# Order of the first normalisation, of the last q tile and of the reciprocal loads in an adaLN block with linear attention and SwiGLU

## The chip, the cores and the metric

The kernel runs on one core of a Trainium2 chip. The metric is the device time of one execution in microseconds, the median of several. All times below are in microseconds (us) unless they are marked ns.

## The reference

One block of a conditioned transformer over 2048 tokens of 1024 features, in bf16: an adaptive layer norm, linear attention with 32 heads of 32 features, a gated residual, a second adaptive layer norm, a SwiGLU feed-forward part with 3584 hidden features, and a second gated residual.

```python
def _layernorm(x, axis=-1, eps=1e-05):
    m = jnp.mean(x, axis=axis, keepdims=True)
    v = jnp.var(x, axis=axis, keepdims=True)
    return (x - m) / jnp.sqrt(v + eps)

def _A_ref(x, wqkv, wo):                     # H = 32 heads
    q, k, v = heads_of(x @ wqkv)
    phi = lambda t: jnp.where(t > 0, t + 1, jnp.exp(t)) + 1e-06
    pq, pk = (phi(q), phi(k))
    kv = jnp.einsum('bhsd,bhse->bhde', pk, v)
    z = jnp.einsum('bhsd->bhd', pk)
    num = jnp.einsum('bhqd,bhde->bhqe', pq, kv)
    den = jnp.einsum('bhqd,bhd->bhq', pq, z)[..., None] + 1e-06
    return merge(num / den) @ wo

def _B_ref(x, w_gate, w_up, w_down):
    return _silu(x @ w_gate) * (x @ w_up) @ w_down

x = A_x
mod = (_silu(c) @ w_mod).reshape(c.shape[0], 6, 1, -1)
sa, ca, ga, sb, cb, gb = (mod[:, i] for i in range(6))
h = _layernorm(x, axis=-1) * (1 + ca) + sa
x = x + ga * _A_ref(h, A_wqkv, A_wo)
h = _layernorm(x, axis=-1) * (1 + cb) + sb
x = x + gb * _B_ref(h, B_w_gate, B_w_up, B_w_down)
```

(`heads_of` and `merge` stand here for the reshapes and transposes.)

## The kernel before

**Engines and order.** Every instruction goes through a small recorder, the class `_Prog`. It appends it to the list of its engine, works out from the memory it touches which earlier instructions it must wait for, and later emits the five lists with semaphore waits. So each engine works in exactly the order in which the Python code calls it, and all lines of the profile are the recorder's line 176. SP issues nearly all DMAs in the order of the calls; `P.wait_for("sp", ...)` makes SP stand until the named instructions are done, and whatever is queued on SP behind it stands too. A PSUM bank is guarded as a whole: an engine that touches it waits for the last access of the other engines.

**Tiling.** The 2048 tokens are 16 row tiles of 128 and four chunks of 512. The 1024 features are 8 tiles of 128, called `dt` where they are summed over and `nt` where they are made. `XRES` holds x and then its norm, `HT` two chunks of h transposed (features on the partitions), `WQK` and `WV` the weights, `PQT` phi(q) transposed, `PKT` and `PKH` phi(k).

**Head.** SP loads row tiles 0 to 3, then the weights of the modulation and of q. TensorE runs filler products (`warm`) on a zeroed tile. Tiles 0 and 2 get mean and variance on VectorE (`s0_`, `s2_`: two halves with `bn_stats`, then an aggregate), tiles 1 and 3 on ScalarE (`act_stats`: a pass for the sum, a pass for the squares; `msq_neg` and `ve_sums` make the variance). POOL computes (variance + eps) to the power −1/2 for one tile at a time (`ln1_rstd1`, `pool_pow`), VectorE applies the norm (`ln1_xn`, `ln1_xn_sum`), and TensorE turns the tile into PSUM with eight products against the identity (`tile_transposes`). Between the turns, `mod_sc` computes columns of the scale 1 + ca: 8 products of one column for each feature tile `m`. `fin_ca` writes them to `MODCOL`, and `h0_first` scales the turned tiles into `HT`.

**q of chunk 0** (`q_phase_chunk0`). The sum over `dt` is taken in pieces for q tiles 0 to 6, each in its own PSUM bank (`qb`), as weights and scales arrive; the shift sa is computed meanwhile (`mod_sc(WSA, ...)`), all in bank 0. Features 0 to 3 enter without their shift, and the missing share is put into a bias (`bias_mm`, `bias_fin`), after which `h0_shift` adds the shift to `HT`. The eighth q tile (`nt` 7) has no bank left: it comes last, in bank 0, after the bias has been read from it. `q_phi` evacuates each tile twice on ScalarE (exp and relu, with the bias), `q_min` and `q_add` make phi(q) from them on VectorE. In the same stretch the rows 4 to 7 of chunk 1 are normalised and transposed by DMA (`th_dma`).

**k, and chunks 1 to 3.** `k_group` and `q_group` make one tile of k or q with eight products of 512 columns; `next_bank` gives the bank in a fixed rotation. `kside`, `s1`, `s2` and `s3` are lists written out by hand: which other work is called after which group. `th_mod` applies scale and shift to a transposed chunk, `ln_half` computes sums for a later chunk, `macc` sums another part of the modulation.

**G and the attention output.** `g_group` makes G = x normᵀ · phi(k) in 16 groups, `g_evac` writes each. `den` computes the denominators, writes their reciprocals to DRAM (`RDR`) and reads them back, each row broadcast to 32 partitions, into `RB`: eight DMAs in two groups of four feature tiles. `scale_pq` multiplies phi(q) by `RB`, one feature tile after each of the groups 7 to 14. `kvt_mm` and `m_mm` fold v and wo into the matrix `MW`, so that the attention output is one product of `PQT` with `MW` (`wo_part`, `wo_res`). `STGX` stages further modulation weights over the place of `RB`. From some 200 us on the feed-forward part runs; no edit touches it.

Of the kernel before, what the change touches and what calls it, by code (L numbers as in the profile page):

```python
# [262 lines left out]
def bass_adaLN_cond__linear_attn_block__swiglu_ffn__prompt_kernel(  # L263
# [22 lines left out]
    with ExitStack() as es:  # L286
# [59 lines left out]
        RL = T("rl", 188 * KB, [128, 4, 512], BF16)  # L346
        E1X = T("e1x", 192 * KB, [128, 4, 512], BF16)
        RLX = T("rlx", 196 * KB, [128, 4, 512], BF16)
        ACC = T("acc", 192 * KB, [128, D], FP32)
        MHL = T("mhl", 196 * KB, [128, 2, D], BF16)  # L350
        MHLT = T("mhlt", 192 * KB, [128, 2 * NDT, 128], BF16)
# [273 lines left out]
                  op0=ALU.add, op1=ALU.add)  # L625
            pool_pow(st)

        warm(13, bank=3)
        act_stats(1)
        act_stats(3)  # L630
        for f in s0_:
# [1 line left out]
        ln1_rstd1(0)  # L633
        msq_neg(1)
        s2_[0]()
        ln1_xn(0)
        tile_transposes(0)
        warm(5, bank=3)
        ve_sums(1)
        s2_[1]()  # L640
        s2_[2]()
        ln1_rstd1(2)
        ln1_xn_sum(1)
        tile_transposes(1)
        warm(1, bank=3)
        msq_neg(3)
        ln1_xn(2, 0, 512)
        ve_sums(3)
        ln1_xn(2, 512, D)
        tile_transposes(2)  # L650
        mod_sc(WCA, 8, range(2))
        ln1_xn_sum(3, 0, 512)
        ln1_xn_sum(3, 512, D)
        fin_ca(0, 2)
        tile_transposes(3)
        mod_sc(WCA, 8, range(2, 4))
        h0_first(0, "dve")
        h0_first(1, "dve")
        raw_copy(4, "dve")
# [43 lines left out]
        def next_bank():  # L703
            i = qk_ctr[0]
            qk_ctr[0] += 1
            return (1, 2, 3, 4, 6, 7, 5, 0)[i % 8] if i < 40 else i % 5 + 1

        def q_group(ch, nt):
            buf, bank = ch % 2, next_bank()
# [39 lines left out]
        def mod_row_b(bank, i, dst):  # L749
# [3 lines left out]
            P.wait_for("sp", [wr])  # L753
            P.dma("mdr%d" % i, dst[:], MDR[i].unsqueeze(0).to_broadcast([128, D]))

        def q_slot(nt):
            return (E1, RL) if nt < 4 else (E1X, RLX)

        def q_phi(nt, bank):
            for buf, fn_ in zip(q_slot(nt), (ACT.Exp, ACT.Relu)):  # L760
                P.act("activation", out=buf[:, nt % 4, :], in_=PS[:, bank, :], func=fn_, bias=BIASQ[:, nt:nt + 1])

        def q_min(nts):
            for nt in nts:
                e = q_slot(nt)[0][:, nt % 4, :]
                P.dve("tensor_scalar", out=e, in0=e, scalar1=1.0, scalar2=1e-6, op0=ALU.min, op1=ALU.add)

        def q_add(nts):
            for nt in nts:
                e, r = q_slot(nt)  # L770
                P.dve("tensor_tensor", out=PQT[:, nt, 0:512], in0=r[:, nt % 4, :], in1=e[:, nt % 4, :], op=ALU.add)

        def q_phase_chunk0():
            qb = [1, 2, 3, 4, 6, 7, 5]
            fin_ca(2, 2)
# [12 lines left out]
            act_stats(4, (0,))  # L788
            for nt in range(7):
                if nt == 6:  # L790
                    mod_sc(WSA, 0, range(6, 8))
                    fin_sa(6, 2)
                    for dt in (6, 7):
                        h0_scale(dt)
                q_part(nt, qb[nt], (4, 5))
            mod_sc(WSA, 0, range(4, 6))
            fin_sa(4, 2, True)
            for dt in (4, 5):
                h0_shift(dt)
            for nt in range(7):  # L800
                if nt == 2:
                    bias_mm((4, 5))
                q_part(nt, qb[nt], (6,))
            for nt in range(7):
                if nt == 1:
                    mod_sc(WSA, 0, range(4), range(4))
                if nt == 3:
                    mod_sc(WSA, 0, range(4), range(4, 8))
                    fin_sa(0, 4, True)
                    ln_ops[1][0]()  # L810
                if nt == 5:
                    bias_mm(range(4))
                    bias_fin()
                q_part(nt, qb[nt], (7,))
            ln_ops[1][1]()
            ln_ops[1][2]()
            ln1_rstd1(5)
            for i, dt in enumerate((4, 5, 0, 1, 2, 3, 6, 7)):
                P.pe("matmul", out=PS[:, 0, :], lhsT=WQK[:, dt, 896:1024], rhs=HT[:, 0, dt, :], start=(i == 0),
                     stop=(i == 7))  # L820
            for dt in range(4):
                h0_shift(dt)
            ln1_xn(5)
# [8 lines left out]
            act_var(4)  # L832
            pool_pow(4)
            for f in ln_ops[3]:
                f()
            ln1_rstd2(6)
            ln1_xn_sum(4)
            th_dma(4)
            q_min((0, 1))
            for st in (6, 7):  # L840
                ln1_xn(st)
                th_dma(st)
            q_add((0, 1))
            for nts in ((2, 3), (4, 5)):
                q_min(nts)
                q_add(nts)
            qk_ctr[0] = 0

        def add(d, k, f):
# [120 lines left out]
        def den():  # L970
            for hg in range(NHG):
                for ch in range(NCH):
                    P.pe("matmul", out=PS[32 * ch:32 * ch + 32, 7, :], lhsT=ZSEL[:, hg * 32:hg * 32 + 32],
                         rhs=PQT[:, hg, ch * 512:(ch + 1) * 512], start=(hg == 0), stop=(hg == NHG - 1),
                         skip_group_check=True)
            P.dve("tensor_scalar", out=DEN[:], in0=PS[:, 7, :], scalar1=1e-6, scalar2=None, op0=ALU.add)
            P.dve("reciprocal", out=RCP[:], in_=DEN[:])
            P.dve("tensor_copy", out=RCB[:], in_=RCP[:])
            wr = [P.dma("rdr%d" % ch, RDR[:, ch * 512:(ch + 1) * 512], RCB[32 * ch:32 * ch + 32, :])
                  for ch in range(NCH)]  # L980
            P.wait_for("sp", wr)
            for gh in range(2):
                outs = [RB[32 * hh:32 * hh + 32, 4 * gh:4 * gh + 4, :] for hh in range(4)]
                ins = [RDR.rearrange("(g x) s -> x g s", x=4)[hh, 4 * gh:4 * gh + 4].unsqueeze(0).to_broadcast([32, 4, S])
                       for hh in range(4)]

                def fn(e, outs=outs, ins=ins):
                    return [e.dma_start(out=o_, in_=i_) for o_, i_ in zip(outs, ins)]

                P.add("sp", fn, reads=[], writes=outs, lane="rb%d" % gh, ninc=4, tag="rb")  # L990
# [4 lines left out]
        def kvt_mm(half):  # L995
            for h in range(4):
                for dt in range(NDT):
                    for g in range(4):
                        c0 = 512 * half + 128 * g + 32 * h
                        P.pe("matmul", out=PS[32 * g:32 * g + 32, 6, 32 * h:32 * h + 32], lhsT=WV[:, dt, c0:c0 + 32],  # L1000
                             rhs=G[:, dt, c0:c0 + 32], start=(h == 0 and dt == 0), stop=(dt == NDT - 1),
                             skip_group_check=True)
            P.dve("tensor_copy", out=KVT[:, half, :], in_=PS[:, 6, 0:128])

        def m_mm(half, nh, banks):
            for k in range(4):
# [31 lines left out]
        for g in range(16):  # L1038
# [209 lines left out]
```

## Time and profile before

| what | us |
|---|---|
| median of 3 runs (lowest, highest) | 827.69 (827.62, 828.37) |
| the profiled execution's own time | 827.71 |
| its span, first to last instruction | 826.0 |
| idle time of TensorE in 0 to 12 | 2.72 |
| first product of q (`ps<-ht,wqk`) | 11.99 |
| VectorE's waits for `rb`, one in all | 6.6 |

The time of an execution has 1.7 us that lie outside the span. The profile counts an engine as busy from the start of an instruction to its end; products on TensorE overlap, so what tells of its pace is the step from start to start: 0.216 for a product of 512 columns in a full stream. A few product records are missing in the trace, and each leaves a step of 0.43 that is none.

### The profile page before, as it was taken

How to read it: one execution, taken by the hardware profiler on the slowest of the kernel's cores; microseconds unless marked ns; L12 is line 12 of the kernel's file. 1: busy time of each engine (PE TensorE's matmuls, PEld its weight loads, DVE VectorE, ACT ScalarE, POOL GpSimd, SP SyncE). 2: the span in 40 equal slices, each digit the busy share in tenths (PEclk: the TensorE clock that was granted, in tenths of full speed). 3: DMA queues.
4: the chain of work that ended last, by engine and by line, in shares of the span. 5: the costliest groups of instructions: out<-in, count | busy, mean ns of one | idle time of the engine just before them, and what ended most of it. 6: DMA issues, size and time to landing. Idle time of an engine off the chain costs nothing.

```text
span 826.0 us, 10436 instructions
## 1 busy us (share of the span) xinstructions
PE 816.3 (99%) x4243; PEld 375.9 (46%) x4322; DVE 312.2 (38%) x672; ACT 197.0 (24%) x338; POOL 41.0 (5%) x58
## 2 busy tenths in 40 slices
PE   8999999999999999999999999999999999999998
PEld 4544444444444444444444444444444444444444
DVE  5798988477945521111221112122111111221111
ACT  4758642123341111011111101111110111111011
POOL 1110000000130000020000003000000300000000
DMA  9969756865698995600455570045557004553000
GB/s 316 297 139 223 167 159 149 181 175 211 149 253 245 296 249 153 166 26 26 136 151 151 153 174 25 23 131 153 151 152 182 27 19 126 151 152 88 0 26 26
DMA packets 199392, 119.32 MB, mean 144 GB/s; under 512 B 58024, under 2 KB 183088, under 8 KB 199344
## 3 DMA queue, kind: packets, MB, share of 16 engines
q1 hardware_dynamic: 199328, 118.65, 53.8%
q8 instruction: 34, 0.56, 0.3%
q14 instruction: 14, 0.11, 0.0%
q10 hardware_dynamic: 16, 0.00, 0.0%
HBM read 100.67 MB, written 4.33 MB: 127 GB/s over the span
## 4 chain that ended last, share of the span: by engine, by line
PE 98%; issue 1%; DMA 0%; DVE 0%; POOL 0%; SPq 0%
PE ps L176 98%; DMA xres<-in_A_x_dram 0%; POOL rstd L176 0%; DVE xres L176 0%; DVE stats L176 0%; SPq L176 0%; DVE ht L176 0%; DVE ve L176 0%; DVE mv L176 0%; DVE modcol L176 0%
## 5 line engine op out<-in xcount | busy, mean ns | idle before, releaser
L176 PE MATMUL ps<-h2t,gug 128*128 128x512 bf16 x878 | 210.1, 379 | 0.9
L176 PE MATMUL ps<-h2t,guu 128*128 128x512 bf16 x878 | 209.9, 379 | 0.9
L176 DVE TENSOR_TENSOR at<-sg,ps 128x512 bf16<-128x512 bf16 x112 | 77.0, 687 | 282.8 <-PE ps L176 270.6
L176 ACT ACTIVATE sg<-ps 128x512 bf16<-128x512 f32 x112 | 66.9, 597 | 309.7 <-PE ps L176 298.3
L176 PEld LDWEIGHTS ps<-h2t,guu 128*128 128x128 bf16 x896 | 87.7, 98 | 105.7
L176 PEld LDWEIGHTS ps<-h2t,gug 128*128 128x128 bf16 x896 | 87.6, 98 | 105.5
L176 PE MATMUL ps<-wd_a,at 128*128 128x512 bf16 (+1 forms) x502 | 111.9, 377 | 0.5
L176 PE MATMUL ps<-ht,wqk 128*128 128x512 bf16 x499 | 110.7, 379 | 0.9 <-DVE ht L176 0.2
L176 PE MATMUL ps<-wd_b,at 128*128 128x512 bf16 (+1 forms) x377 | 84.6, 377 | 0.4
L176 PEld LDWEIGHTS ps<-wd_a,at 128*128 128x128 bf16 x512 | 50.1, 98 | 59.6
L176 DVE TENSOR_TENSOR ut<-att,gb_b 128x512 bf16<-128x512 bf16 (+1 forms) x32 | 13.6, 426 | 167.5 <-ACT att L176 167.5
L176 PEld LDWEIGHTS ps<-ht,wqk 128*128 128x128 bf16 x512 | 49.2, 98 | 58.9 <-DVE ht L176 1.0
L176 ACT ACTIVATE att<-ps 128x512 bf16<-128x512 f32 (+1 forms) x32 | 17.4, 591 | 182.1 <-PE ps L176 182.1
L176 PEld LDWEIGHTS ps<-wd_b,at 128*128 128x128 bf16 x384 | 37.6, 98 | 44.7
L176 PE MATMUL ps<-pk,xres 128*128 128x512 bf16 x250 | 55.4, 379 | 0.6 <-issue 0.5
L176 PE MATMUL ps<-mw,pqt 128*128 128x512 bf16 x249 | 55.4, 379 | 0.5 <-issue 0.2
L176 POOL TENSOR_SCALAR h2t<-h2t,modcol 128x512 bf16<-128x512 bf16 x32 | 26.5, 846 | 383.0 <-DMA h2t<-xn 383.0
L176 ACT ACTIVATE e<-ps 128x512 bf16<-128x512 f32 x56 | 33.3, 611 | 31.8 <-PE ps L176 15.8
L176 ACT ACTIVATE junk<-xres 128x1024 bf16<-128x1024 bf16 x26 | 27.6, 1063 | 45.9 <-DVE xres L176 34.2
L176 PEld LDWEIGHTS ps<-mw,pqt 128*128 128x128 bf16 x256 | 24.8, 98 | 30.0 <-issue 0.5
L176 PEld LDWEIGHTS ps<-pk,xres 128*128 128x128 bf16 x256 | 24.6, 98 | 30.1 <-issue 1.3
L176 DVE SCALAR_TENSOR_TENSOR xres<-ps,xres 128x512 bf16<-128x512 f32 x32 | 21.5, 688 | 11.6 <-PE ps L176 11.3
(111 smaller groups left out, 337.8 us busy)
## 6 DMA issues: line engine op xcount, KB each, us to landing
gug<-in_B_w_gate_dram SPq DMA_DIRECT2D x56, 512.0 KB, 4.0
guu<-in_B_w_up_dram SPq DMA_DIRECT2D x56, 512.0 KB, 5.3
xres<-in_A_x_dram SPq DMA_DIRECT2D x20, 256.0 KB, 4.4
rb<-recip_den SPq DMA_DIRECT2D x8, 512.0 KB, 11.7
stgx<-in_w_mod_dram SPq DMA_DIRECT2D x2, 2048.0 KB, 9.3
wd_a<-in_B_w_down_dram SPq DMA_DIRECT2D x4, 1024.0 KB, 7.7
out_dram<-xres SPq DMA_DIRECT2D x31, 128.0 KB, 1.7
xres<-in_A_x_dram SPq DMA_DIRECT2D x3, 1024.0 KB, 6.5
```

Source lines behind the costliest of these rows:

```text
L176: return getattr(e, method)(**kw)
```

## The change

Four parts of the code change.

The head: the sums and the variance of tile 2 are finished before tile 0 is normalised; there is one filler more at the start and three instead of six between the turns; the scale columns of three feature tiles, instead of two, are computed ahead of the turns of tile 3.

The last q tile: q tile 0 is complete first and is copied out of its bank by ScalarE to a new fp32 tile, `QRAW`; `nt` 7 takes that bank, and its eight products are spread around the shift and bias products. The order of the evacuation becomes 1 to 7, then 0. Row tile 4 gets its sums, its root, its norm and its transposing DMA earlier.

The lists: the rotation of banks begins at 0 instead of 1 and has a changed order in chunk 2; `th_mod` of chunk 1 comes in 12 pieces instead of 16; the last four q tiles are finished after the fourth k group instead of the second; sums, norms and DMAs of chunk 3 are called later.

The reciprocals: `RB` is loaded in three groups (3, 3 and 2 feature tiles), and the third is issued only after `kvt_mm(0)`; the last two calls of `scale_pq` move from the groups 13 and 14 to 14 and 15.

```diff
-        warm(13, bank=3)
+        warm(14, bank=3)
         act_stats(1)
         act_stats(3)
         for f in s0_:
@@
         msq_neg(1)
         s2_[0]()
+        s2_[1]()
+        ve_sums(1)
+        s2_[2]()
+        ln1_rstd1(2)
         ln1_xn(0)
         tile_transposes(0)
-        warm(5, bank=3)
-        ve_sums(1)
-        s2_[1]()
-        s2_[2]()
-        ln1_rstd1(2)
+        warm(1, bank=3)
         ln1_xn_sum(1)
         tile_transposes(1)
-        warm(1, bank=3)
+        warm(2, bank=3)
         msq_neg(3)
...
         tile_transposes(2)
-        mod_sc(WCA, 8, range(2))
+        mod_sc(WCA, 8, range(3))
         ln1_xn_sum(3, 0, 512)
         ln1_xn_sum(3, 512, D)
-        fin_ca(0, 2)
+        fin_ca(0, 3)
         tile_transposes(3)
-        mod_sc(WCA, 8, range(2, 4))
+        mod_sc(WCA, 8, range(3, 4))
@@ next_bank
-            return (1, 2, 3, 4, 6, 7, 5, 0)[i % 8] if i < 40 else i % 5 + 1
+            if i < 24:
+                return (0, 2, 3, 4, 6, 7, 5, 1)[i % 8]
+            if i < 40:
+                return (0, 2, 3, 4, 6, 1, 7, 5, 0, 2, 3, 1, 4, 6, 7, 5)[i - 24]
+            return i % 5 + 1
@@
+        QORD = (1, 2, 3, 4, 5, 6, 7, 0)
...
+        def q_pair(i):
+            q_min(QORD[i:i + 2])
+            q_add(QORD[i:i + 2])
@@ q_phase_chunk0
-            act_stats(4, (0,))
...
             for nt in range(7):
-                if nt == 1:
+                q_part(nt, qb[nt], (7,))
+                if nt == 0:
+                    P.act("activation", out=QRAW[:], in_=PS[:, qb[0], :], func=ACT.Copy)
+                    act_stats(4)
+            for i, dt in enumerate(range(NDT)):
+                if i == 1:
                     mod_sc(WSA, 0, range(4), range(4))
-                if nt == 3:
+                if i == 3:
                     mod_sc(WSA, 0, range(4), range(4, 8))
+                    ln_ops[1][0]()
                     fin_sa(0, 4, True)
-                    ln_ops[1][0]()
-                if nt == 5:
+                    ln_ops[1][1]()
+                    act_var(4)
+                    pool_pow(4)
+                if i == 5:
                     bias_mm(range(4))
                     bias_fin()
-                q_part(nt, qb[nt], (7,))
-            ln_ops[1][1]()
+                P.pe("matmul", out=PS[:, qb[0], :], lhsT=WQK[:, dt, 896:1024], rhs=HT[:, 0, dt, :], start=(i == 0),
+                     stop=(i == 7))
             ln_ops[1][2]()
             ln1_rstd1(5)
-            for i, dt in enumerate((4, 5, 0, 1, 2, 3, 6, 7)):
-                P.pe("matmul", out=PS[:, 0, :], lhsT=WQK[:, dt, 896:1024], rhs=HT[:, 0, dt, :], start=(i == 0),
-                     stop=(i == 7))
             for dt in range(4):
                 h0_shift(dt)
+            ln1_xn_sum(4)
+            th_dma(4)
             ln1_xn(5)
             th_dma(5)
-            for nt in range(2):
-                q_phi(nt, qb[nt])
-            act_stats(4, (1,))
-            for nt in range(2, 8):
-                q_phi(nt, qb[nt] if nt < 7 else 0)
+            for nt in QORD:
+                q_phi(nt, QRAW[:] if nt == 0 else PS[:, qb[nt % 7], :])
...
@@ kside
-        for c0 in (0, 256):
-            for dt in range(NDT):
-                add(kside, 1, lambda dt=dt, c0=c0: th_mod(1, dt, c0, c0 + 256))
-        add(kside, 1, lambda: q_min((6, 7)))
-        add(kside, 1, lambda: q_add((6, 7)))
-        for jj, k in ((0, 3), (1, 4)):
+        for dt, c0, c1 in ([(dt, 0, 256) for dt in range(4)] + [(dt, 256, 512) for dt in range(4)]
+                           + [(dt, 0, 512) for dt in range(4, 8)]):
+            add(kside, 1, lambda dt=dt, c0=c0, c1=c1: th_mod(1, dt, c0, c1))
+        for i in (4, 6):
+            add(kside, 3, lambda i=i: q_pair(i))
+        for jj, k in ((0, 4), (1, 5)):
@@ s1, s2
-        ln_half(3, s1, 8, 8, 11)
+        ln_half(3, s1, 12, 12, 14)
         for jj in range(4):
-            add(s1, 13 + jj // 2, lambda jj=jj: ln1_xn(12 + jj))
-            add(s2, 0, lambda jj=jj: th_dma(12 + jj))
+            add(s1 if jj < 2 else s2, 15 if jj < 2 else 0, lambda jj=jj: ln1_xn(12 + jj))
+            add(s2, 1, lambda jj=jj: th_dma(12 + jj))
@@ den
-            for gh in range(2):
...
+            rb_load(0, 3)
+            rb_load(3, 6)
+
+        def rb_load(h0, h1):
+            outs = [RB[32 * x:32 * x + 32, h0:h1, :] for x in range(4)]
...
+            P.add("sp", fn, reads=[], writes=outs, lane="rb%d" % h0, ninc=4, tag="rb")
@@ the loop over g
             if g == 10:
-                kvt_mm(0)
+                P.wait_for("sp", [kvt_mm(0)])
+                rb_load(6, 8)
             if 11 <= g < 13:
                 m_mm(0, g - 11, [MB, 7, G_BANKS[4], 6])
-            if 7 <= g < 15:
+            if 7 <= g < 13:
                 scale_pq(g - 7)
+            elif g == 14:
+                scale_pq(6)
+            elif g == 15:
+                scale_pq(7)
```

More of the change, by code (lines that the diff above doesn't have):

```diff
@@ L348, in bass_adaLN_cond__linear_attn_block__swiglu_ffn__prompt_kernel @@
         RLX = T("rlx", 196 * KB, [128, 4, 512], BF16)
+        QRAW = T("qraw", 202 * KB, [128, 512], FP32)
         ACC = T("acc", 192 * KB, [128, D], FP32)
@@ L754, in mod_row_b, with q_phi @@
             P.dma("mdr%d" % i, dst[:], MDR[i].unsqueeze(0).to_broadcast([128, D]))
+        QORD = (1, 2, 3, 4, 5, 6, 7, 0)
         def q_slot(nt):
-            return (E1, RL) if nt < 4 else (E1X, RLX)
-        def q_phi(nt, bank):
+            i = QORD.index(nt)
+            bufs = (E1, RL) if i < 4 else (E1X, RLX)
+            return [t[:, i % 4, :] for t in bufs]
+        def q_phi(nt, src):
             for buf, fn_ in zip(q_slot(nt), (ACT.Exp, ACT.Relu)):
-                P.act("activation", out=buf[:, nt % 4, :], in_=PS[:, bank, :], func=fn_, bias=BIASQ[:, nt:nt + 1])
+                P.act("activation", out=buf, in_=src, func=fn_, bias=BIASQ[:, nt:nt + 1])
         def q_min(nts):
             for nt in nts:
-                e = q_slot(nt)[0][:, nt % 4, :]
+                e = q_slot(nt)[0]
                 P.dve("tensor_scalar", out=e, in0=e, scalar1=1.0, scalar2=1e-6, op0=ALU.min, op1=ALU.add)
@@ L770, in q_add @@
                 e, r = q_slot(nt)
-                P.dve("tensor_tensor", out=PQT[:, nt, 0:512], in0=r[:, nt % 4, :], in1=e[:, nt % 4, :], op=ALU.add)
+                P.dve("tensor_tensor", out=PQT[:, nt, 0:512], in0=r, in1=e, op=ALU.add)
+        def q_pair(i):
+            q_min(QORD[i:i + 2])
+            q_add(QORD[i:i + 2])
         def q_phase_chunk0():
             qb = [1, 2, 3, 4, 6, 7, 5]
-            fin_ca(2, 2)
+            fin_ca(3, 1)
             for dt in (2, 3):
@@ L804, in q_phase_chunk0 @@
             for nt in range(7):
-                if nt == 1:
+                q_part(nt, qb[nt], (7,))
[4 more added lines that the diff above has]
+                if i == 1:
                     mod_sc(WSA, 0, range(4), range(4))
-                if nt == 3:
+                if i == 3:
                     mod_sc(WSA, 0, range(4), range(4, 8))
+                    ln_ops[1][0]()
                     fin_sa(0, 4, True)
-                    ln_ops[1][0]()
-                if nt == 5:
+                    ln_ops[1][1]()
+                    act_var(4)
+                    pool_pow(4)
+                if i == 5:
                     bias_mm(range(4))
                     bias_fin()
-                q_part(nt, qb[nt], (7,))
-            ln_ops[1][1]()
+                P.pe("matmul", out=PS[:, qb[0], :], lhsT=WQK[:, dt, 896:1024], rhs=HT[:, 0, dt, :], start=(i == 0),
+                     stop=(i == 7))
             ln_ops[1][2]()
             ln1_rstd1(5)
-            for i, dt in enumerate((4, 5, 0, 1, 2, 3, 6, 7)):
-                P.pe("matmul", out=PS[:, 0, :], lhsT=WQK[:, dt, 896:1024], rhs=HT[:, 0, dt, :], start=(i == 0),
-                     stop=(i == 7))
             for dt in range(4):
                 h0_shift(dt)
+            ln1_xn_sum(4)
+            th_dma(4)
             ln1_xn(5)
             th_dma(5)
-            for nt in range(2):
-                q_phi(nt, qb[nt])
-            act_stats(4, (1,))
-            for nt in range(2, 8):
-                q_phi(nt, qb[nt] if nt < 7 else 0)
+            for nt in QORD:
+                q_phi(nt, QRAW[:] if nt == 0 else PS[:, qb[nt % 7], :])
             for f in ln_ops[2]:
                 f()
-            act_var(4)
-            pool_pow(4)
             for f in ln_ops[3]:
@@ L836, in q_phase_chunk0 @@
             ln1_rstd2(6)
-            ln1_xn_sum(4)
-            th_dma(4)
-            q_min((0, 1))
+            q_min(QORD[0:2])
             for st in (6, 7):
@@ L842, in q_phase_chunk0 @@
                 th_dma(st)
[L843 to L846, printed above, removed]
+            q_add(QORD[0:2])
+            q_pair(2)
             qk_ctr[0] = 0
@@ L981, in den, with fn @@
             P.wait_for("sp", wr)
-            for gh in range(2):
[L983 to L990, printed above, removed]
+            rb_load(0, 3)
+            rb_load(3, 6)
+        def rb_load(h0, h1):
+            outs = [RB[32 * x:32 * x + 32, h0:h1, :] for x in range(4)]
+            ins = [RDR.rearrange("(g x) s -> x g s", x=4)[x, h0:h1].unsqueeze(0).to_broadcast([32, h1 - h0, S])
+                   for x in range(4)]
+            def fn(e, outs=outs, ins=ins):
+                return [e.dma_start(out=o_, in_=i_) for o_, i_ in zip(outs, ins)]
+            P.add("sp", fn, reads=[], writes=outs, lane="rb%d" % h0, ninc=4, tag="rb")
         def scale_pq(hg):
@@ L1002, in kvt_mm @@
                              skip_group_check=True)
-            P.dve("tensor_copy", out=KVT[:, half, :], in_=PS[:, 6, 0:128])
+            return P.dve("tensor_copy", out=KVT[:, half, :], in_=PS[:, 6, 0:128])
         def m_mm(half, nh, banks):
```

## The prediction

> **What bounds the kernel now.** I read the page's first part, then the chain that ended last, then busy time by stretch, and only then the single instructions.
>
> ```profile
> span 826.0 us, 10436 instructions
> PE 816.3 (99%) x4243; PEld 375.9 (46%) x4322; DVE 312.2 (38%) x672; ACT 197.0 (24%) x338; POOL 41.0 (5%) x58
> ...
> PE 98%; issue 1%; DMA 0%; DVE 0%; POOL 0%; SPq 0%
> ```
>
> TensorE is the bound, and the chain is TensorE for 98% of the span. So an edit counts only where it starts TensorE's stream earlier, takes instructions out of it or opens a gap in it. Busy time by stretch shows where gaps are:
>
> ```profile
> 0.00:12.00 12.00, 9.28 (x85) 4.97 (x87) 8.55 (x35) 6.56 (x11) 3.30 (x11) 1.00 0.85 283
> 12.00:43.00 31.00, 30.57 (x264) 15.72 (x269) 19.83 (x68) 18.54 (x33) 2.23 (x3) 1.00 1.14 320
> 43.00:125.00 82.00, 81.63 (x375) 36.93 (x381) 74.21 (x206) 50.67 (x92) 4.02 (x8) 1.00 0.73 165
> 125.00:193.00 68.00, 67.15 (x632) 30.89 (x639) 43.59 (x64) 17.32 (x28) 0.00 (x0) 1.00 0.66 161
> ```
>
> The second number is TensorE's busy time: idle are 2.72 us in the first stretch, then 0.43, 0.37 and 0.85. After 12 us all the change could touch is 1.65 us, and most of that is the step from one shape of product to another, which stays. The head is not TensorE's time. Its chain, in order of time:
>
> ```profile
> 1.71 4.05 DMA xres<-in_A_x_dram
> ...
> 7.92 0.17 DVE ve L176
> ...
> 8.16 0.79 POOL rstd L176
> ...
> 9.30 0.22 DVE ve L176
> ...
> 9.59 0.66 POOL rstd L176
> ...
> 10.27 0.42 DVE xres L176
> ...
> 10.74 1.10 PE ps L176 x24
> ...
> 11.99 5.47 PE ps L176 x53
> ```
>
> Row tile 2 lands at 5.76; its sums wait behind the norm of tile 0; its root (8.16) ends at 8.94; then tile 3's root, norm, turns (transposes), 16 narrow products, and the first real product at 11.99. From there the stream is full.
>
> **Part 1, the head.** VectorE's new order from 5.78, with steps from the timeline: first half of tile 2's sums 5.78, second 6.39 (step 0.61, as between the two halves of tile 0 at 3.49 and 4.10), variance of tile 1 at 7.00, tile 2's aggregate 7.11 (0.72 after the second half, as 6.96 to 7.68), its variance 7.36 instead of 7.92, norm of tile 0 at 7.43 instead of 6.39, norm of tile 1 at 7.88 instead of 7.99. So tile 2's variance is 0.56 earlier. How much survives depends on POOL, which computes the roots one by one:
>
> ```profile
> 7.12 0.56 POOL L176 TENSOR_TENSOR rstd<-ve,neghalf 128x1 f32<-128x1 f32 x1 [1.19 <-DVE ve L176]
> 8.16 0.78 POOL L176 TENSOR_TENSOR rstd<-ve,neghalf 128x1 f32<-128x1 f32 x1 [0.47 <-DVE ve L176]
> 9.59 0.65 POOL L176 TENSOR_TENSOR rstd<-ve,neghalf 128x1 f32<-128x1 f32 x1 [0.65 <-DVE ve L176]
> ```
>
> 0.56 beside the sums, 0.78 and 0.65 beside a norm: both longer roots end 0.49 after VectorE is done with the norm (8.45 and 9.75). Tile 1's root would start at 7.00 + 0.28 = 7.28 and end at 7.85. Tile 2's, queued behind it, starts there: it ends at 8.45 if undisturbed (0.56 to 0.60) or, if it is caught by tile 1's norm of 7.89 to 8.41, at 8.41 + 0.49 = 8.90, hardly before today's 8.94. Tile 3's variance is 0.33 after the norm of tile 2 begins (8.97 to 9.30) but not before ScalarE's sum of squares at 8.97, so 9.0 to 9.26 against 9.30. Gain of this chain: 0.04 to 0.30.
>
> [...]
>
> Second term: eight of tile 3's narrow products move ahead of its turns. Sixteen cost the stream 0.40 (21.20 to 21.61), so eight take 0.20 out of what follows the last turn. They need the gap before the turns: 24 products from about 9.9 (their weights land at 9.83 by the landing events) end near 10.5, the turns become possible at 10.4 to 10.7. Bounds 0.06 and 0.20; I take 0.20, because the late case of the root leaves room. Fillers go from 19 to 17; all stand where TensorE waits, so nothing.
> Sum of the head: 0.10 to 0.50 earlier; I take 0.30, between the two ends that the root can have.
>
> **Part 2, the last q tile.** Its eight products (0.216 each) replace other products as cover between the same three groups of narrow products:
>
> ```profile
> 24.61 0.54 PE L176 MATMUL ps<-siluc,wsa 128*128 128x1 bf16 x16
> ...
> 25.45 0.54 PE L176 MATMUL ps<-siluc,wsa 128*128 128x1 bf16 x16
> ...
> 26.34 0.95 PE L176 MATMUL ps<-modtmp,wqk 128*128 128x1 bf16 x32
> ```
>
> Count and changes of shape are the same: nothing in TensorE's time. The added ScalarE copy of q tile 0 (0.6 to 0.7, as one evacuation) lies under six products (1.3 us) before its bank is written again. If that cover went, 0.3. The bias is ready three products before the first k product instead of ten: at 28.3 against 28.8 for k, whose bank it shares. VectorE has queued before it half a tile's sums and tile 4's variance, which waits for two ScalarE passes over a tile that lands at 25.52 (2.35 us as at 4.12 to 6.46, so 27.9): still before 28.3. The four shifts end by 29.9, needed from 29.7 to 30.3; spare 0.4. Bounds 0 to +0.3; I take 0. ScalarE: the second pass over tile 4 leaves its run of sixteen evacuations, which starts 0.8 later and ends at about 37.6 (was 37.77).
>
> **Part 3, chunk 1.** Tile 4's transposing DMA is issued about 30.5 instead of 34.07, ahead of tile 5's, and moves past nothing else on SP. The modulation loses four instructions: eight of 0.257 and four of 0.40 make 3.7 instead of 4.18. It ends near 44.0 and chunk 1 starts 0.3 earlier, at 42.8, needing its last piece at 44.3. Today TensorE loses 0.04 at 44.4 and 0.13 at 46.4 (steps of 252 and 349 ns against 216); the second goes with the two q pairs that are queued behind the next evacuation. Gain 0.1; worst, with transposes landing as late as today's 41.8, minus 0.3.
>
> **Part 4, lists, RB, SP.** Bank order keeps at least five groups (8.6 us) before reuse; LN of chunk 3 moves within VectorE and SP time that TensorE does not wait for. RB: today VectorE sits 6.6 us on the first group (to 161.28) and TensorE feels nothing, since the first reader of its sums comes at 166.4. A first group of 1.5 MB instead of 2 lands about 2 to 3 us earlier: zero. The new SP wait stands ahead of the last RB group, with the 2 MB staging load behind it; the wait ends with the copy at 169.08, the load could not go before 170.5 anyway, and it gets about 5 us of extra queue: landed by 185, needed at 195.8. The last two scalings come at g 14 and 15 with 2.7 us of VectorE idle before the last evacuation. Zero; if late, the second halves of the output products at 191.5 would wait, several us off.
>
> **Sum.** 826.0 − 0.30 − 0.10 = 825.6 in the span. The profiled execution took 827.71, 1.71 outside its span, and that is the median of 827.69. Forecast: 825.6 + 1.7 = **827.3 us**.
>
> **Rivals.**
> *The gain is eaten by landings.* The second group of shift weights lands at 20.48 and is used at 20.99; with products 0.3 to 0.5 earlier the slack is nearly gone, and 0.5 of jitter would give all back. For: DMA is full to 36 us. Against: it fits in this trace. Time 827.6.
> *POOL gives the gain back.* The two roots now stand back to back under two norms. If a root that has begun holds a norm off until it ends, tile 0's norm waits for tile 1's root (7.43 to 7.85), tile 1's norm for tile 2's root, and the chain is 0.35 later, less the 0.20 of products. [...] Time 827.71 + 0.15 − 0.1 = 827.8. [...]
> *Slower: TensorE's clock falls in the head.* The fillers end near 7.15 (one more at 0.216 after 6.93) and the first turn cannot come before 7.95, 0.8 us of nothing where today five fillers and turns follow at once. The first fillers step at 0.427, from 2.61 to 5.57, the later ones at 0.216. If the pace fell for a stretch as long (2.96), real products would lose half of it, 1.48, and the sixteen turns on the path 0.056 each, 0.9: 827.7 + 2.4 − 0.4 = 829.7. It decides once idle 0.8 us is enough for a fall. Against: today's kernel goes from 9.3 to 11.99 with turns and narrow products alone and comes out at 0.216.
> [...]
> *Chunk 1 starved*, or a late RB: 828.3.
> *That TensorE's stream gains over 1.65 us* has no source in these windows except a different start.
>
> **Numbers.** Forecast 0.63, landings 0.12, POOL 0.12, clock 0.08, starved 0.03, unknown gain 0.02. A measurement here tells about 0.2%, 1.65 us, from no change: faster needs under 826.0, slower over 829.35. Faster 0.04, same 0.87, slower 0.09. Range 826.4 to 828.7: the forecast's own 826.9 to 827.6, the two give-backs, the starved case, and drift of the runs (827.62 to 828.37).
>
> **What would show it.** Tile 2's root ending at 8.45 or 8.90; first real product at 11.5 to 11.9; first k product 0.3 earlier than 29.31; no step over 0.25 at 44.4 and 46.4; the rest of the chain unchanged and shifted. A step of 0.427 after 7 us, a wait on the shift weights, or any gap of TensorE between 160 and 193 that is not a change of shape would prove me wrong.

## The result and the profile after

| | before | after |
|---|---|---|
| median of 15 runs each, side by side on one chip (lowest, highest) | 828.01 (827.59, 828.50) | 829.47 (828.78, 829.99) |
| the profiled execution's own time | 827.71 | 829.99 |
| its span | 826.0 | 828.3 |

The ratio is 1.0017, with an interval of 1.0010 to 1.0024: the changed kernel is 1.46 us slower. The forecast of 827.3 and its range to 828.7 were both missed, on the slow side.

The first part of the page after and its line on the chain that ended last:

```profile
span 828.3 us, 10512 instructions
PE 821.0 (99%) x4320; PEld 376.0 (45%) x4320; DVE 311.9 (38%) x668; ACT 197.4 (24%) x339; POOL 40.8 (5%) x58
...
PE 93%; DVE 4%; DMA 2%; issue 0%; SPq 0%; ACT 0%
```

TensorE was 98% of the chain; now it is 93%, and VectorE and DMA have 6% together. That does not mean 6% of waiting: the chain follows whatever released TensorE, and once it goes over to VectorE it stays there until VectorE itself was released. It says where to look. Busy time of the engines by stretch, after (start and end, length, then busy time on TensorE, its weight loads, VectorE, ScalarE, POOL; granted clock, DMA share, GB/s):

```profile
0.00:12.00 12.00, 8.35 (x70) 4.36 (x71) 7.71 (x32) 6.06 (x10) 3.30 (x11) 1.00 0.84 282
12.00:43.00 31.00, 30.77 (x280) 15.94 (x278) 17.94 (x59) 18.29 (x31) 2.00 (x3) 1.00 1.16 311
43.00:125.00 82.00, 80.83 (x376) 36.23 (x374) 72.83 (x203) 50.65 (x93) 3.96 (x8) 1.00 0.71 169
125.00:193.00 68.00, 68.00 (x627) 31.18 (x626) 45.20 (x70) 17.34 (x28) 0.00 (x0) 1.00 0.63 161
```

Two stretches have idle time of TensorE that they should not have: the head (3.65 against 2.72) and 43 to 125 (1.17 against 0.37). The 0.37 of before is not even idle time: that trace has 4243 products for 4322 weight loads, and its seven gaps of 0.05 there stand where records are missing. The trace of after has them all (4320 and 4320).

**The account by products.** The same weight load of the same product can be looked up in both traces, and the difference of their starts runs along the stream. It is +1.02 at the first q product (weight loads at 11.74 and 12.76; the 11.99 of the trace of before is its second product, for the record of the first is missing), +1.03 at 43, +0.83 from 48 to 113, +1.67 at 117 and +2.36 from 121 to the end. So the profiled execution lost 1.02 in the head, won back 0.2 at the start of chunk 1, and lost 0.82 and 0.68 at two places in chunk 3.

The loss of 1.02 is mostly this one execution, the slowest of the fifteen. Chain of the head, in order of time (start, duration, what):

```profile
2.65 8.47 DMA wca<-in_w_mod_dram
...
11.17 1.01 PE ps L176 x28
12.18 0.48 DVE ht L176
...
12.79 1.24 PE ps L176 x5
```

The first group of scale weights landed at 11.12. In the twelve other profiled executions of this study it landed between 9.45 and 10.08. The two steps in chunk 3 are the change's own. Timeline of VectorE there, before (start, duration, operation, output from input; in brackets how long VectorE stood before it, and for what):

```profile
104.50 2.29 DVE L176 TENSOR_REDUCE red<-mhlt 128x8 f32<-128x2048 bf16 x1
...
110.83 0.75 DVE L176 TENSOR_SCALAR acc<-stg,siluf 128x1024 f32<-128x1024 bf16 x1 [2.22 <-DMA stg<-in_w_mod_dram]
...
111.90 0.68 DVE L176 SCALAR_TENSOR_TENSOR pkt<-ps,e 128x512 bf16<-128x512 f32 x1
...
116.05 0.68 DVE L176 SCALAR_TENSOR_TENSOR pkt<-ps,e 128x512 bf16<-128x512 f32 x1
```

and after, with TensorE's timeline of the same time below it:

```profile
107.93 2.29 DVE L176 TENSOR_REDUCE red<-mhlt 128x8 f32<-128x2048 bf16 x1 [1.72 <-DMA mhlt<-mhl]
...
113.95 0.75 DVE L176 TENSOR_SCALAR acc<-stg,siluf 128x1024 f32<-128x1024 bf16 x1 [1.91 <-DMA stg<-in_w_mod_dram]
...
115.02 0.68 DVE L176 SCALAR_TENSOR_TENSOR pkt<-ps,e 128x512 bf16<-128x512 f32 x1
...
119.16 0.68 DVE L176 SCALAR_TENSOR_TENSOR pkt<-ps,e 128x512 bf16<-128x512 f32 x1
```

```profile
111.27 3.84 PE L176 MATMUL ps<-ht,wqk 128*128 128x512 bf16 x17
115.77 3.63 PE L176 MATMUL ps<-ht,wqk 128*128 128x512 bf16 x16 [0.66 <-DVE pkt L176]
119.91 1.47 PE L176 MATMUL ps<-ht,wqk 128*128 128x512 bf16 x6 [0.51 <-DVE pkt L176]
```

VectorE now stands twice: 1.72 for the transposed modulation sums (`mhlt`, read by the reduction `mod_red`) and 1.91 for the staged weights (`stg`). Before, it stood for the second alone. The rows `pkt<-ps,e` at 115.02 and 119.16 are the evacuations of the k tiles 4 and 6 of chunk 3. They are queued behind those stands, and the second and fourth q group of the chunk take the banks of these two tiles: TensorE starts at 115.77 and 119.91, right behind them.

**A limit that can be read off.** Call lag the time from the last weight load of a tile's products to VectorE's start on it. Before, the evacuation of k tile 4 had a lag of 5.13 and ended at 112.58, and its bank was next written at 114.10: 1.52 to spare, so the largest lag that costs nothing is 5.13 + 1.52 = 6.65. Tile 6 had a lag of 5.83 before, and so 0.82 to spare. After, the lags of tiles 4 and 6 are 7.42 and 8.10. By the limit the first loses 0.77 (0.82 measured); the second, which the first has already put off by 0.82, loses 8.10 − 6.65 − 0.82 = 0.63 (0.68 measured).

### The profile page after: what moved, and what is told of

It is laid out like the page before. It is cut to its first block, busy times and chain, and to the rows that moved or that the text cites. A ratio compares the mean times of both kernels' runs of the same rounds, so it can differ in the third digit from the quotient of the medians.

```text
span 828.3 us, 10512 instructions
## 1 busy us (share of the span) xinstructions
PE 821.0 (99%) x4320; PEld 376.0 (45%) x4320; DVE 311.9 (38%) x668; ACT 197.4 (24%) x339; POOL 40.8 (5%) x58
## 4 chain that ended last, share of the span: by engine, by line
PE 93%; DVE 4%; DMA 2%; issue 0%; SPq 0%; ACT 0%
PE ps L176 93%; DVE acc L176 1%; DMA wca<-in_w_mod_dram 1%; DMA stg<-in_w_mod_dram 1%; DVE pkt L176 1%; DVE e L176 1%; DVE pqt L176 0%; SPq L176 0%; DVE xres L176 0%; DVE mhl L176 0%; DVE ht L176 0%; ACT e L176 0%; ACT rl L176 0%; ACT junk L176 0%
```

## The experiments

Each kernel ran eleven times unless another number is given, beside the kernel before on the same chip. The reference medians of before were 828.41 for the first four kernels, 828.16 for the next four and 828.20 for the last three.

### The old lists for chunk 3 in the changed kernel

```diff
-        ln_half(3, s1, 12, 12, 14)
+        ln_half(3, s1, 8, 8, 11)
         for jj in range(4):
-            add(s1 if jj < 2 else s2, 15 if jj < 2 else 0, lambda jj=jj: ln1_xn(12 + jj))
-            add(s2, 1, lambda jj=jj: th_dma(12 + jj))
+            add(s1, 13 + jj // 2, lambda jj=jj: ln1_xn(12 + jj))
+            add(s2, 0, lambda jj=jj: th_dma(12 + jj))
```

> The changed kernel with one part undone: the lists for the norm of chunk 3 (sums, norms, transposing DMAs) are called where they were before. Theory (late lists: VectorE carries some 3 us more backlog through chunk 2, so that two groups of chunk 3 wait for their bank, 0.82 and 0.68 us at 114.7 and 119.0): both steps fall to 0.216, the first k evacuation of chunk 2 lags about 5.5 us behind its products instead of 8.8, and the time falls by 1.5 to 827.9 to 828.1 (ratio to before 0.9995 to 1.0002). Rival 1 (the new bank order alone makes the two waits): the waits stay, 829.5. Rival 2 (the head with its late first product costs it): the waits may go but the time stays over 829.

Measured: 828.61, ratio 1.0003 (0.9994 to 1.0011). The steps at 114 and 119 are gone, and the late lists are their cause. But the kernel does not come out at the expected 827.9 to 828.1, because another wait appears, at the start of chunk 2. TensorE, then ScalarE's two last scalings of chunk 2 in this kernel:

```profile
72.68 3.68 PE L176 MATMUL ps<-ht,wqk 128*128 128x512 bf16 x15 [0.30 <-ACT ht L176]
```

```profile
71.80 1.53 ACT L176 ACTIVATE ht<-ht,modcol 128x512 bf16<-128x512 bf16 x2
```

and the same row in the changed kernel:

```profile
69.41 1.52 ACT L176 ACTIVATE ht<-ht,modcol 128x512 bf16<-128x512 bf16 x2
```

Two products step by 683 and 474 ns instead of 216, together 0.72 lost. With the old lists, sums over chunk 3's rows stand on ScalarE and VectorE among the scalings of chunk 2, and the changed kernel reaches this place later than the one before (its evacuations in chunk 1 run 1.1 us further behind their products, with two q pairs put after the fourth k group). This is read from the two traces; the new list for chunk 1 was not undone alone. So the late lists buy 0.7 at 72 and pay 1.5 at 114 to 120.

### The late lists alone, in the kernel before

The same edit the other way round, in the old kernel.

> The kernel before with one part done alone: the later lists for the norm of chunk 3. Theory (late lists): steps of 0.7 to 1.0 us appear in chunk 3 near 114 and 118 and the time rises by 1.2 to 1.5, to 829.2 to 829.5. Rival 1 (bank order) and rival 2 (head): 828.0, no such step.

Measured: 829.81, ratio 1.0018 (1.0009 to 1.0027), a little over the expected 829.2 to 829.5. The lists alone cost about what the whole change costs. Lags of tiles 4 and 6: 6.85 and 7.54; by the limit 0.20 and, less the 0.27 lost before it, 0.62; the steps at 114.28 and 118.01 lost 0.27 and 0.68. The profiled execution lost another 1.2 further on; VectorE and TensorE there:

```profile
163.99 1.23 DVE L176 TENSOR_TENSOR pqt<-pqt,rb 128x2048 bf16<-128x2048 bf16 x1 [7.99 <-DMA rb<-recip_den]
```

```profile
175.19 1.04 PE L176 MATMUL ps<-pk,xres 128*128 128x512 bf16 x4 [1.07 <-issue]
```

The reciprocals, in the old two groups, landed 2.7 later than in the trace of before (161.3), VectorE took up its scalings that much later, and a bank of `G` came free too late. This too follows from VectorE's lateness. The second reduction of the modulation, which waits for its transposed sums in the same way, starts at 136.16 instead of 133.78, the denominators queued behind it at 138.97 instead of 136.59, and the loads are issued at 152.15 instead of 149.30, while TensorE's own stream is only 1.4 later at 133. The row names "issue"; that the bank was what it waited for is read from the order of VectorE's evacuations (the last of them ends at 175.06) and was not tried apart.

### A longer bank distance in the changed kernel, two ways

```diff
+            if i < 56:
+                return (0, 2, 3, 1, 4, 6, 7, 5, 0, 2, 3, 1, 4, 6, 5, 7)[i - 40]
             return i % 5 + 1
```

> The changed kernel with one thing added: the banks of chunk 3 come round after seven or eight groups instead of five; all lists stay as changed. Theory (late lists, felt only because a bank is due again after five groups, 8.6 us): VectorE is as late as in the changed kernel, yet the two waits are gone, 827.9 to 828.1. If the late VectorE were felt in another way (the sum of the modulation, the reduction at 108): 829 or more. Rival 2 (head): 829 or more.

Measured in five runs: 834.49, ratio 1.0078 (1.0064 to 1.0092), far over either expectation. The waits at 114 and 119 went, with VectorE as late as before. But I had put the last q group on bank 7, which a row of the modulation occupies until VectorE has copied it:

```profile
128.69 3.48 PE L176 MATMUL ps<-ht,wqk 128*128 128x512 bf16 x8 [4.27 <-DVE mr L176]
```

Eight products take 3.48, so they ran at half pace: their steps are 0.40 to 0.43 against 0.216, and the granted clock from 128.6 to 132.2 is 0.54 (0.998 in the mean of the execution). The bank was my own error. The same edit with bank 3 for the last group:

> The changed kernel with banks of chunk 3 that come round after five to eight groups, and bank 7 left alone from the time at which the gate row of the modulation uses it. Theory (late VectorE, felt through banks that are due again after five groups): VectorE as late as in the changed kernel (k evacuations of chunk 2 lag 8.8 us at first), no wait at 114 and 119, no other wait, 827.7 to 828.1, that is 1.4 to 1.8 under the changed kernel's 829.47. Rival (the late VectorE costs TensorE its time in another place, at the end of chunk 3): waits of the same sum elsewhere, 829 or more.

Measured: 827.62, ratio 0.9994 (0.9985 to 1.0003), just under the expected range. VectorE's two evacuations, and TensorE:

```profile
114.68 0.68 DVE L176 SCALAR_TENSOR_TENSOR pkt<-ps,e 128x512 bf16<-128x512 f32 x1
...
118.83 0.68 DVE L176 SCALAR_TENSOR_TENSOR pkt<-ps,e 128x512 bf16<-128x512 f32 x1
```

```profile
111.71 9.44 PE L176 MATMUL ps<-ht,wqk 128*128 128x512 bf16 x43
```

The lags are 7.93 and 8.62, more than in the changed kernel, and TensorE runs through without a pause. That VectorE is late costs nothing by itself; that the bank is due again after five groups makes it cost. Tile 4's bank is due after eight groups here, which moves the limit by three groups of 1.73.

### The reduction two groups later, its sums one

```diff
-            add(s3, 4 + kt, lambda kt=kt: macc(STG, kt))
+            add(s3, 5 + kt, lambda kt=kt: macc(STG, kt))
...
-        s3.setdefault(2, []).extend([mod_red, mod_row_a])
+        s3.setdefault(4, []).extend([mod_red, mod_row_a])
```

> The changed kernel with the reduction of the modulation called two k groups later in chunk 3 and the eight sums behind it one group later, so that VectorE does not stand on their transfers with evacuations queued behind. Theory (of the lateness that bites at 114.7 and 119.0, VectorE's two stands on transfers, 1.72 at 107.9 and 1.91 at 113.9, are the larger part): both waits of TensorE shrink to 0.3 or less together, 828.0 to 828.4. Rival (it is the number of VectorE instructions, not the stands): the waits only move later, 829.3.

Measured: 827.57, ratio 0.9993 (0.9984 to 1.0001), lower than the expected 828.0 to 828.4. VectorE:

```profile
107.70 2.28 DVE L176 TENSOR_REDUCE red<-mhlt 128x8 f32<-128x2048 bf16 x1
...
113.28 0.75 DVE L176 TENSOR_SCALAR acc<-stg,siluf 128x1024 f32<-128x1024 bf16 x1 [1.48 <-DMA stg<-in_w_mod_dram]
...
115.67 0.68 DVE L176 SCALAR_TENSOR_TENSOR pkt<-ps,e 128x512 bf16<-128x512 f32 x1
```

The amount of work is the same. The reduction starts without a stand, one more pair of evacuations goes ahead of it and one ahead of the stand of 1.48 that is left: lags of 3.82 and 5.54, under the limit, and no step of TensorE over 0.28 between 12 and 132.

The same edit in the kernel before with the late lists:

> The kernel before with the later lists for chunk 3 and, beside them, the reduction and its sums one k group later. The theory (late lists cost only through VectorE standing on the reduction's transfers) expects the loss gone here too: 827.9 to 828.3, no step over 0.3 us at 114 to 120, lag of the evacuations of the fourth and sixth k group of chunk 2 under 6 us. Rival (late lists cost TensorE through the amount of VectorE work that they push into chunk 3): 829.3 to 829.9 as with the late lists alone.

Measured: 828.23, ratio 1.0000 (0.9991 to 1.0009), against 829.81 without it. Lags of tiles 4 and 6 of chunk 3: 3.82 and 4.23, nothing at 114 to 120. The denominators are back at 136.63, and the 1.2 at 175 is gone as well. So the cause holds in both kernels: not the late lists' work, but where VectorE stands for transfers that they make late.

### The reciprocals alone, in the kernel before

Three loads instead of two, the third behind `kvt_mm(0)`, and the last two scalings moved, as in the diff of the change.

> The kernel before with the reciprocals loaded in three groups, the third behind the copy of group 10, and the last two scalings later: this part alone. Prediction: no difference, 828.0 to 828.4. Rival, from one run of the kernel with late lists, where TensorE waited 1.2 us at 173.7 behind a late first group: the change takes such waits away, first scaling at about 158 to 161 instead of 161 to 164, and the median falls by 0.1 to 0.5. A new wait by SP's order would show as a gap between 183 and 193.

Measured: 828.02, ratio 0.9998 (0.9989 to 1.0007). All scalings by `rb` on VectorE, what they waited for (us, times):

```profile
  DMA rb<-recip_den: 4.8, 1
```

The first scaling starts at 159.4 instead of 161.3. TensorE's products are where they were (−0.02), with no gap from 160 to 193. The median is 0.14 under its reference, which both the prediction and its rival allow: the trace says that nothing was gained here, the times alone cannot.

### The head alone, and the change without the head

The head of the change in the old kernel:

> The kernel before with the new order of the head alone (tile 2's sums ahead of the norms, 14 and 3 fillers, three scale columns ahead of tile 3's turns). Forecast of the prediction: 0.1 to 0.5 faster than before, 827.5 to 827.9, first product of q at 11.5 to 11.9 when the first scale weights land at 9.8. Rival 2 (the head makes the loss): 829 or more, first product at 12.7. A middle reading (POOL gives the gain back, or the landing of the scale weights sets the start): 828.0, and the first product about 1.6 after that landing.

Measured: 827.87, ratio 0.9995 (0.9986 to 1.0004). The old head in the changed kernel:

> The changed kernel with the head as before. If the new head gains what the prediction says, 0.1 to 0.5 slower than the changed kernel: 829.6 to 830.0. If the landings of the weights give its gain back, the same: 829.3 to 829.6. If the new head costs, 829.2 or less. The first product of q at 11.9 to 12.1 in the first two cases when the first scale weights land at 9.8.

Measured: 829.84, ratio 1.0018 (1.0010 to 1.0027), against 829.47 with the new head. And the old head where nothing behind it stalls, that is with the later reduction:

> The changed kernel with the old head and with the reduction one k group later, so that the head can be sized where nothing behind it stalls. The theory (the head is worth the 0.2 to 0.5 us of the forecast) expects 827.8 to 828.1 against 827.57 with the new head, first q product 0.2 to 0.5 us later at equal landings. Rival (the landings of the scale and shift weights give the gain of the head back): 827.4 to 827.7, the same as with the new head.

Measured: 827.95, ratio 0.9999 (0.9990 to 1.0008), against 827.57. The medians of all three pairs give the new head 0.4 to 0.5, their ratios, each to its own reference, 0.1 to 0.5; but each interval is some 0.75 us to either side, so this is a sign and no size. The traces are clearer on the parts. From the landing of tile 2 to the end of tile 3's root it takes 4.58 in the mean of the six kernels with the old head (4.48 to 4.71) and 4.35 in the seven with the new one (4.15 to 4.49): 0.23 gained. The first product's weight load, though, comes 0.80 to 0.82 after VectorE begins to write the first scale columns, in all thirteen. With the old head the narrow products behind the turns end at about the same time (the weight load follows them without a gap in four kernels, after 0.09 in two), so there both set it. With eight of them gone, the scale columns alone do. TensorE in the kernel with the later reduction:

```profile
10.26 0.74 PE L176 MATMUL ps<-siluc,wca 128*128 128x1 bf16 x24
10.86 0.61 PE L176 MATMUL ps<-ident,xres 128*128 128x128 bf16 x8
11.30 0.34 PE L176 MATMUL ps<-siluc,wca 128*128 128x1 bf16 x8
11.87 1.46 PE L176 MATMUL ps<-ht,wqk 128*128 128x512 bf16 x6 [0.23 <-DVE ht L176]
```

TensorE is done with the narrow products and stands 0.23 for VectorE's first scaling (`ht`), which follows the scale columns. Those wait for all 24 products ahead of the turns, eight more than before. Behind tile 3's root they come 0.16 later than with the old head, in the mean (0.80 and 0.96, without the execution whose weights landed at 11.12), and most of the 0.23 is spent again: counted from the landing of tile 2, the first weight load comes at 6.20 in the mean with the old head and at 6.11 with the new.

The eight products are not all of that 0.16, and they were not moved alone. In five of these twelve executions, two with the old head and three with the new, the fillers stepped at 0.427 for so long that the turns of tile 0 came straight behind them, and TensorE was late from there on: the scale columns come 0.81 and 1.26 after the root with the old head and 0.96 to 1.31 with the new. In the other seven it is 0.68 to 0.69 and 0.71 to 0.89, and the first weight load comes at 6.09 and 5.86 from the landing. So in these few executions the head is worth some 0.2 where the fillers end in time, and less where they do not.

### Both cures together

> The changed kernel with both cures at once: the reduction and its sums one k group later, and the longer bank distance in chunk 3. The theory (the 1.5 us of steps at 114 and 119 are one loss, and either cure takes all of it) expects no more from two than from one: 827.3 to 827.8, span 825.5 to 826.0, no step of a product over 0.3 us between 70 and 130, first k evacuation lag in chunk 2 under 6 us. Rival (each cure left a part of its own behind): 826.6 to 827.1.

Measured: 827.86, ratio 0.9996 (0.9987 to 1.0005). Two cures do no more than one. The expected lag of under 6 was wrong: the first k evacuation of chunk 2 still lags by 8.83, for both cures act in chunk 3. It costs nothing, as that bank is due again only after eight groups. No kernel with a cure is told apart from the kernel before; the lowest is the one with the later reduction alone.

## Why the prediction failed

**The step that failed** is Part 4: "Bank order keeps at least five groups (8.6 us) before reuse; LN of chunk 3 moves within VectorE and SP time that TensorE does not wait for." I compared 8.6 us with nothing. The time to the last weight load of the group itself (1.3) and the evacuation (0.68) come off it, and what remains for lag is 6.65. The trace of before already showed lags of 5.13 and 5.83 at these two tiles, and a stand of 2.22 on the staged weights a little ahead of them. With the change the sums (`macc`) start at 84.76 instead of 80.62 (83.27 with the late lists alone); the transposed sums land at 107.91 instead of 104.48 and the staged weights at 113.92 instead of 110.81. The reduction stays at its place in the list. So VectorE waits where it did not, and two evacuations wait with it. I had costed the moved normalisations as work on an engine with time to spare and did not follow the moved steps to the transfers that come out of them. In medians this is worth 1.9 us: 829.47 against 827.57 and 827.62 with either cure. The two steps in the trace make 1.5; the intervals, 0.6 and 0.75 to either side, cover the difference.

A reading ahead of it was wrong too, without weight for the result: the idle 0.37 and 0.85 after 43 us are not steps between shapes of products but missing records, and the trace of after, which has all records, shows 68.00 busy of 68.00 from 125 to 193.

**Part 1, the head.** The root chain was right: 0.23 in a bracket of 0.04 to 0.30. POOL took neither of the two cases. Its roots, after:

```profile
7.50 1.35 POOL L176 TENSOR_TENSOR rstd<-ve,neghalf 128x1 f32<-128x1 f32 x2 [1.49 <-DVE ve L176]
9.79 0.65 POOL L176 TENSOR_TENSOR rstd<-ve,neghalf 128x1 f32<-128x1 f32 x1 [0.93 <-DVE ve L176]
```

The two back to back take 0.73 and 0.82 where they took 0.56 and 0.78. Tile 2's ends at 8.85, which looks like the forecast 8.90 by luck: tile 2 landed at 6.00 here instead of 5.76. Counted from the start of its sums the root ends after 2.83, before it was 3.16, and the two cases were 2.67 and 3.12. The norms beside them take 0.54 and 0.55, hardly more than before (0.53 and 0.54); each root ends 0.04 after the norm that began beside it. So a root beside a norm is stretched, by 0.17 and 0.25 over the undisturbed 0.56, and VectorE is not stopped. The trace of before shows the same beside four shifts: they start at 28.44 and keep steps of 0.26, while the root beside them takes 0.74:

```profile
28.44 1.13 DVE L176 TENSOR_SCALAR ht<-ht,modcol 128x512 bf16<-128x512 bf16 x4
...
28.61 0.74 POOL L176 TENSOR_TENSOR rstd<-ve,neghalf 128x1 f32<-128x1 f32 x1 [18.37 <-DVE ve L176]
```

The second term, 0.20 for eight narrow products, was wrong and is 0 or less, for the reason above: I took the products behind the turns for the only path, and another of the same length ran through the scale columns. The fillers, put at nothing, held up the turns in five executions.

**Part 2** held. The difference between the traces is +1.02 before the shift products and +1.03 at 43, and each group of sixteen still takes 0.54:

```profile
27.15 0.54 PE L176 MATMUL ps<-siluc,wsa 128*128 128x1 bf16 x16
...
27.98 0.54 PE L176 MATMUL ps<-siluc,wsa 128*128 128x1 bf16 x16
```

**Part 3** held, with 0.2 instead of 0.1: the steps at 44.4 and 46.4 are gone, while the kernels with the old lists for chunk 1 still show 349 to 352 ns at 46 to 47. What I did not see is the price: the evacuations run 1.1 us further behind, which, as far as the traces show, is what the old chunk 3 lists stumble on at 72. It shows in chunk 3 as well: tile 4's lag is 6.85 with the late lists alone and 7.42 in the changed kernel.

**The reciprocals and the SP wait** cost nothing and gave nothing in the traces, as forecast. The old two groups had less to spare than I took them to have: in the kernel with the late lists alone the scalings began 2.7 later and TensorE's stream ran 1.4 later, and these 1.3 between them cost 1.2. So next to nothing was spare. Whether three groups guard against that was not tried with such a landing.

**The rivals.** *Landings* happened, in single executions: with the head alone the second shift weights landed at 21.56 and TensorE's step at 20.99 was 0.62. *POOL* stretched but did not turn the gain round: the norm of tile 0 begins at 7.66, under a root that runs from 7.50 to 8.23. No run shows a norm that is held off until a root ends, which is what the 0.35 of that sum stood on. *The clock* did not fall in the head, though TensorE had steps of up to 1.04 there: the q products behind them step at 0.215 to 0.216. That its 829.7 came nearest to the measured time is chance. A fall was measured in one place: after the idle 4.27 us in the kernel with the bank error, eight products at half pace cost 1.6 (3.31 from the first to the next product behind them, less 8 × 0.216). So steps of 1.04 were not followed by a fall here, and 4.27 us without work were; what lies between was not tried. *Chunk 1 starved* did not happen. The rival that was missing is the one that came: an engine with spare time that stands in front of somebody's evacuation.

## What to carry to other kernels

Where engines work in the order of their lists, moving work later also moves every transfer that comes out of it, and the reader of that transfer stays where it was: follow a moved step to its last reader, and look at what is queued behind that reader. For each evacuated bank, compute the largest lag (the time until the bank is written again, less the evacuation) and compare it with the lag in the trace; an engine that is 38% busy can still be 0.8 us from stopping TensorE. If it is too close, a longer bank distance or the waiting reader a group or two later can cure it (827.62 and 827.57 here, against 829.47), and neither removes any work.

## What the runs showed of the hardware

**TensorE's first half pace has no fixed length.** The fillers start at 2.6 or at 2.9 to 3.0 and step by 0.427 instead of 0.216 until some time between 5.5 and 8.1, in kernels whose heads are the same. The granted clock reads 1.00 there all the same (from 2 to 8 before, from 2 to 9 after), so only the steps tell of it. In the kernel with both cures it lasted to 8.1; the first turns followed at 8.5, though VectorE had finished the norm of tile 0 at about 7.9, and it then stood for the narrow products:

```profile
11.28 0.16 DVE L176 TENSOR_SCALAR modcol<-ps 128x3 f32<-128x3 f32 x1 [0.40 <-PE ps L176]
```

I had counted fillers as free in every execution. **Landings scatter more than the edits are worth**: the first scale weights, issued at 2.65 each time, land between 9.45 and 11.12. A head that is worth 0.2 cannot be read from one profile, and its median not from eleven runs.
